# The weights of neighbouring tokens made by VectorE from token rows instead of by TensorE, in a fused RWKV-6 and MLP-mixer kernel

## The chip, the cores and the metric

The kernel runs on one core of a Trainium2 chip. The metric is the device time of one execution in microseconds. Before the change it is 612.65 us, the median of three runs (612.45, 612.65 and 614.34). The profiled execution took 611.08 us and its recorded span is 609.3 us; all times inside the program below are counted from the start of that span.

## What is computed

The reference, cut to what matters. There are 4 batches, 8 heads, 768 tokens and 48 channels for each head; everything is float32.

```python
# attention: state is (B, H, 48, 48)
for t in range(S):
    kt, vt, rt, wt = k[:, :, t], v[:, :, t], r[:, :, t], w[:, :, t]
    cur = einsum('bhd,bhe->bhde', u[None] * kt, vt)      # the own token, weighted by u
    y[:, :, t] = einsum('bhd,bhde->bhe', rt, state + cur)
    state = wt[..., None] * state + einsum('bhd,bhe->bhde', kt, vt)
# then, on x = y laid out as (B, S, 384): the mixer
h  = relu(x^T @ w_tok1) @ w_tok2        # over tokens, 768 -> 256 -> 768
u_ = x + h^T
out = u_ + relu(u_ @ w_ch1) @ w_ch2     # over channels, 384 -> 1536 -> 384
```

The recurrence is computed in chunks of 64 tokens. Within a chunk the output of token t is a weighted sum of the values of the tokens up to t. The weight of an earlier token s is the sum over channels of r at t, k at s and the decays between them; the weight of the token itself is the sum of r, u and k of this token.

## The kernel before

The work is cut into 12 units of 256 tokens, three for each batch. A unit has 2 blocks of 128 tokens (c), each with two chunks of 64 (j), and 4 pairs of heads (a, with q for the two heads of a pair). r, k and w come in turned: the channels of the two heads of a pair lie on partitions 0 to 47 and 64 to 111, and the tokens run along the free dimension.

The weights within a chunk are made in six levels, with block sizes 1, 2, 4, 8, 16 and 32. At each level TensorE multiplies the left half of every pair of blocks (k) with the right half (r), a copy keeps those results that belong to the level, and `join` multiplies the decays into r and k, so that the next level can work with blocks twice as large. The first level is special: it also makes the weight of each token with itself, for which ScalarE first writes copies of r and k, half of whose columns are multiplied by u.

```python
def begin():                                  # ScalarE: rp, kp
    ...
    for t, x, o in both:
        act.copy(t[:, :, o], x[:, :, o])                                    # L226
    for t, x, o in both:
        ...
        for a in range(A):
            act.mul(t[:, :, a, :], x[:, :, a, :], u_col[:ROWS, a:a + 1])    # L230

def gram0(c): ...                             # L242: products of kp and rp in 64 x 64 tiles
def pick0(c):                                 # L248: VectorE keeps the blocks of two
    dve.copy_predicated(out=at_c[:, :, c, :, :], data=g, mask=masks[0]...)

def join(l, w, new):
    ...
    dve.tensor_mul(left, left, wv[:, :, 1]...to_broadcast([ROWS, n, b]))    # L297, k
    dve.tensor_mul(right, right, wv[:, :, 0]...to_broadcast([ROWS, n, b]))  # L298, r
    dve.tensor_mul(new[:ROWS], wv[:, :, 0], wv[:, :, 1])                    # L299

def first_block():
    join(0, products[0], products[1])
    for c in range(UC):
        gram0(c)
        pick0(c)

def block(l):                                 # l = 1 to 5
    gram(l)                                   # L265 (L259 for the last)
    join(l, products[l], products[l + 1])
    pick(l)                                   # L281 on VectorE, L276 and L289 on ScalarE
```

When the weights of a unit are there, `post` finishes it: `tokens` turns k with TensorE (L331), `carry` makes the products of k and v of each chunk (L341), `update` carries the state from chunk to chunk, `before` multiplies r with the states (L378), `within` multiplies the weights with v (L391).

```python
def update():
    ...
    for c in range(UC):
        for j in range(2):
            ...
            if g == 0:
                dve.tensor_copy(new, got)
            else:
                for a in range(A):
                    dve.scalar_tensor_tensor(new[:, a], state[bt, g][:, a], L["w"][:, c, a, j:j + 1],
                                             got[:, a], op0=ALU.mult, op1=ALU.add)      # L358
```

The mixer of one batch runs beside the attention of the next: its full-size products (L429, L436, L456, L490) are woven with the pieces of the attention in the order of TensorE. `beside` says which of the small products of two units go behind each other; the levels run one unit ahead.

```python
return [(1.0, begin[1]), tokens, one(carry, first), update, one(before, rest[0]), one(within, rest[1]),
        *loads, *rest[2:]]
```

Of the kernel before, what the change touches and what calls it, by code (L numbers as in the profile page):

```python
# [10 lines left out]
f32 = mybir.dt.float32  # L11
# [4 lines left out]
ALU = mybir.AluOpType  # L16
AF = mybir.ActivationFunctionType

B, H, S, D = 4, 8, 768, 48
DM = H * D  # L20
T = 64
C = S // 128
UC = 2
UB = C // UC
NU = B * UB
A = H // 2
P = 64
ROWS = P + D
LEVELS = 6
COLS = UC * A * 128  # L30
DTOK, DCH = 256, 1536
NJ = DCH // 128
PIECE = 512
SEG = 256
HJ, HM = NJ // 2, DM // 2
# [19 lines left out]
def rwkv6_then_mixer(  # L55
    ctx: ExitStack,
    tc: tile.TileContext,
    rkw: bass.AP,
    v: bass.AP,
    u: bass.AP,  # L60
    w_tok1: bass.AP,
    w_tok2: bass.AP,
    w_ch1: bass.AP,
# [15 lines left out]
    pe, dve, act, pool, sp = nc.tensor, nc.vector, nc.scalar, nc.gpsimd, nc.sync  # L79

    block = nc.cur_bb.bb
# [17 lines left out]
    ps_m = ctx.enter_context(tc.tile_pool(name="ps_m", bufs=2, space=bass.MemoryType.PSUM))  # L99


    rs = [const.tile([128, COLS], f32, name=f"r{i}") for i in range(3)]
    ks = [const.tile([128, COLS], f32, name=f"k{i}") for i in range(3)]
    ws = [const.tile([128, COLS], f32, name=f"w{i}") for i in range(3)]
    weights_at = [const.tile([128, 2, UC * A, T], f32, name=f"at{i}") for i in range(3)]
    vs = {}
# [1 line left out]
    def load_rkw(i):  # L108
        if i >= NU:
            return  # L110
        for n, t in enumerate((rs[i % 3], ks[i % 3], ws[i % 3])):
            for rows in (slice(0, 128),) if i < 3 else (slice(0, D), slice(P, P + D)):
                sp.dma_start(t[rows], rkw[i, n, rows, :])
# [7 lines left out]

    u_col = const.tile([128, A], f32, name="u_col")
    act.dma_start(u_col, u)
    load_rkw(0)
    load_rkw(1)

# [2 lines left out]
    masks = []  # L129
    for l in range(4):  # L130
        b = 1 << l
        m = const.tile([128, 64 // b, 2 if l == 0 else b], f32, name=f"mask{l}")
        pool.memset(m, 1.0)
        pool.affine_select(out=m, in_=m, compare_op=ALU.is_ge, fill=0.0, base=0,
                           pattern=[[-2 * b, 64 // b], [0, m.shape[2]]], channel_multiplier=1)
        pool.affine_select(out=m, in_=m, compare_op=ALU.is_ge, fill=0.0, base=b - 1,
                           pattern=[[2 * b, 64 // b], [1 if l == 0 else 0, m.shape[2]]], channel_multiplier=-1)
        n, x = (T, 1) if l == 0 else (32, UC * A)
        m8 = const.tile([128, x, n], u8, name=f"mask8_{l}")
        flat = m.rearrange("p n b -> p (n b)")  # L140
        for j in range(2):
            dve.tensor_copy(m8[ts(j, T)], flat[ts(j, T), ts(j, n)].unsqueeze(1).to_broadcast([T, x, n]))
        masks.append(m8)
    for i, t in enumerate(weights_at):
        (dve if i == 0 else pool).memset(t, 0.0)
    ident = const.tile([128, 128], f32, name="ident")
# [56 lines left out]
    state = {}  # L203


    def levels(i):
# [7 lines left out]
        def begin():  # L214
            decay = apool.tile([128, COLS // 2], f32, name="decay")
            L["w"] = apool.tile([128, UC, A, 2], f32, name="w_chunk", bufs=4)
            pool.memset(L["w"], 0.0)
            products.extend([w_, decay, w_[:, :COLS // 4], decay[:, :COLS // 8], w_[:, :COLS // 16],
                             decay[:, :COLS // 32], L["w"].rearrange("p c a j -> p (c a j)")])

            rp = L["rp"] = apool.tile([128, COLS], f32, name="rp")
            kp = L["kp"] = apool.tile([128, COLS], f32, name="kp", bufs=1)
            both = [(t.rearrange("p (n two) -> p n two", two=2)[:ROWS], x.rearrange("p (n two) -> p n two", two=2)[:ROWS], o)
                    for t, x, o in ((rp, r_, 1), (kp, k_, 0))]
# [3 lines that stand above are left out]
                t, x = (e[:, :, 1 - o].rearrange("p (c a n) -> p c a n", c=UC, a=A) for e in (t, x))  # L228
                for a in range(A):
                    act.mul(t[:, :, a, :], x[:, :, a, :], u_col[:ROWS, a:a + 1])  # L230
# [60 lines left out]
        def join(l, w, new):  # L291
            b = 1 << l
            n = COLS // (2 * b)
            right = r_.rearrange("p (n two b) -> p n two b", two=2, b=b)[:ROWS, :, 1, :]
            left = k_.rearrange("p (n two b) -> p n two b", two=2, b=b)[:ROWS, :, 0, :]
            wv = w.rearrange("p (n two) -> p n two", two=2)[:ROWS]
            dve.tensor_mul(left, left, wv[:, :, 1].unsqueeze(2).to_broadcast([ROWS, n, b]))  # L297
            dve.tensor_mul(right, right, wv[:, :, 0].unsqueeze(2).to_broadcast([ROWS, n, b]))  # L298
            dve.tensor_mul(new[:ROWS], wv[:, :, 0], wv[:, :, 1])  # L299

        def first_block():
# [7 lines left out]
            join(l, products[l], products[l + 1])  # L309
            pick(l)  # L310

        pieces = [(0.1, begin), (1.6, first_block)]
        for l in range(1, LEVELS):
            pieces.append((1.2, lambda l=l: block(l)))
        return pieces

    def post(i):
        bt, half = divmod(i, UB)
# [25 lines left out]
        def update():  # L344
            L = live[i]
            kv = L.pop("kv")
            for c in range(UC):
                for j in range(2):
                    g = 2 * (half * UC + c) + j
                    if g == 2 * C - 1:  # L350
                        continue
                    new = apool.tile([128, A, D], f32, name="state", bufs=6)
                    got = kv[:, j, ds(c * A * D, A * D)].rearrange("p (a e) -> p a e", a=A)
                    if g == 0:
                        dve.tensor_copy(new, got)
                    else:
                        for a in range(A):
                            dve.scalar_tensor_tensor(new[:, a], state[bt, g][:, a], L["w"][:, c, a, j:j + 1], got[:, a],  # L358
                                                     op0=ALU.mult, op1=ALU.add)
                    state[bt, g + 1] = new  # L360


# [177 lines left out]
        downs = [first if (bt, s) == (0, 0) else quarters(s) for s in range(S // SEG)]  # L540
        return hiddens, turned, ups, downs

    def beside(after, ahead):

        tokens, carry, update, before, within, *loads = after
        begin, first, *rest = ahead

        def both(f, g):
            behind = products(f)[-1].name
            for ins in products(g):  # L550
                tc.add_manual_dep(ins, behind, no_sync, reason="products in tiles together")

        def one(*pieces):
            return (sum(c for c, _ in pieces), lambda: both(*(f for _, f in pieces)))


        return [(1.0, begin[1]), tokens, one(carry, first), update, one(before, rest[0]), one(within, rest[1]),
                *loads, *rest[2:]]


    hiddens, turned, ups, downs = mixing(0)
# [16 lines left out]
    for bt in range(B):  # L578
# [13 lines left out]
        if n < NU:  # L592
            att = levels(n) if bt == 0 else []
            for i in range(n, n + UB):
                att += beside(post(i), levels(i + 1)) if i + 1 < NU else post(i)
            emit(woven(att, pieces))
        else:
            emit(pieces)
# [29 lines left out]
```

## Time and profile before

| What | Value |
|---|---|
| time, median of three runs | 612.65 us |
| span of the profiled execution | 609.3 us |
| TensorE busy | 578.8 us |
| VectorE busy | 341.1 us |
| ScalarE busy | 201.1 us |
| first level on TensorE (L242) | 18.0 us busy, 768 records |
| copies and u-scalings on ScalarE (L226, L230) | 48.2 us busy |
| state steps on VectorE (L358) | 30.8 us busy, 160 operations |

The page of a profile gives the busy time of each engine, then the same in 40 equal slices, where each digit is the busy share of a slice in tenths. A row of the list of groups names the line, the engine, the operation, what it writes and reads, the shapes and the number of records; behind the bar stand the busy time in us, the mean of one in ns, and the time the engine stood idle before these operations, with what ended it. A float32 product leaves two records on TensorE. The chain that ended last is followed back from the last instruction: its pieces are what set the end. PE is TensorE's products, PEld its weight loads, DVE is VectorE, ACT ScalarE, POOL GpSimd and SP SyncE, which issues the loads. A busy TensorE is not one at its peak, because the ends of products are modelled.

### The profile page before, as it was taken

To read this page: it belongs to the slowest core of one execution; us is meant where nothing else is said; L and a number is where in the kernel's file an instruction comes from. 1 tells how busy PE (TensorE), PEld (TensorE's weight loads), DVE (VectorE), ACT (ScalarE), POOL (GpSimd) and SP (SyncE) were. 2 spreads that over 40 slices of the span, in tenths; PEclk is the share of its full clock that TensorE was granted. 3 is DMA by queue.
4 is the path that set the end of the run, shared out by engine and by line. 5 is a ranking of instruction groups with operands and counts; after the bars stand their busy time and mean duration, and the time that the engine had idled before them with its cause. 6 is when DMAs were issued, how large, how long until landed. Compare 5 with 4: busy or idle time off the path is not lost.

```text
span 609.3 us, 19865 instructions
## 1 busy us (share of the span) xinstructions
PE 578.8 (95%) x8980; PEld 493.9 (81%) x8980; DVE 341.1 (56%) x743; ACT 201.1 (33%) x500; POOL 7.2 (1%) x32
## 2 busy tenths in 40 slices
PE   3888789999999999999999999999999999999997
PEld 2776567877988886789899896789898896898987
DVE  5889989997666873546364362626254431040403
ACT  6153654530354433442333412332212411303020
POOL 4000000000000000000000000000000000000000
PEclk9997869999999999999999999999999999999999
DMA  8336563610322222111121000000000000000000
GB/s 344 117 81 219 176 191 139 210 65 29 79 84 79 55 68 67 30 52 28 54 54 54 29 28 27 2 2 3 27 2 28 2 28 0 1 14 15 26 1 26
DMA packets 19380, 38.63 MB, mean 63 GB/s; under 512 B 2112, under 2 KB 12864, under 8 KB 19296
## 3 DMA queue, kind: packets, MB, share of 16 engines
q1 hardware_dynamic: 19152, 37.36, 19.0%
q8 instruction: 70, 1.15, 0.8%
q14 instruction: 14, 0.11, 0.1%
q10 hardware_dynamic: 144, 0.00, 0.0%
HBM read 32.64 MB, written 4.72 MB: 61 GB/s over the span
## 4 chain that ended last, share of the span: by engine, by line
PE 85%; DVE 8%; ACT 3%; issue 2%; DMA 1%; SPq 0%; DVEq 0%; ACTq 0%
PE z_ps L456 28%; PE q_ps L490 24%; PE gram L265 8%; PE h_ps L429 6%; PE h_ps L436 5%; PE h_ps L466 3%; PE kv_ps L341 2%; PE y_ps L391 2%; PE y_ps L378 2%; PE gram L331 2%; DVE state L358 2%; PE xT_ps L448 1%; PE gram L242 1%; PE gram L259 1%; DMA w<-in_rkw_dram 1%
## 5 line engine op out<-in xcount | busy, mean ns | idle before, releaser
L456 PE MATMUL z_ps<-xT,wch 128*128 128x256 f32 x864 | 196.1, 382 | 0.1
L456 PEld LDWEIGHTS z_ps<-xT,wch 128*128 128x128 f32 x864 | 160.9, 190 | 22.2 <-ACT z L458 1.0
L458 ACT ACTIVATE z<-z_ps 128x256 f32<-128x256 f32 x144 | 54.9, 382 | 149.4 <-PE z_ps L456 140.5
L490 PE MATMUL q_ps<-wch,z 128*128 128x192 f32 x528 | 94.8, 329 | 0.0
L490 PEld LDWEIGHTS q_ps<-wch,z 128*128 128x128 f32 x528 | 86.1, 190 | 1.4
L265 PEld LDWEIGHTS gram<-r,k 48*64 48x64 f32 x3072 | 59.5, 153 | 13.8 <-issue 7.5
L490 PE MATMUL q_ps<-scratch,z 128*128 128x192 f32 x396 | 70.6, 329 | 0.0
L265 PE MATMUL gram<-r,k 48*64 48x32 f32 x3072 | 64.5, 235 | 5.7 <-issue 2.6
L490 PEld LDWEIGHTS q_ps<-scratch,z 128*128 128x128 f32 x396 | 64.4, 190 | 0.5
L297 DVE TENSOR_TENSOR k<-k,decay 112x512 f32<-112x512 f32 x36 | 24.9, 691 | 44.3 <-PE gram L265 34.5
L482 DVE TENSOR_TENSOR z<-z 128x768 f32<-128x768 f32 x11 | 10.5, 958 | 60.6 <-ACT z L458 60.6
L297 DVE TENSOR_TENSOR k<-k,w 112x512 f32<-112x512 f32 x36 | 24.8, 689 | 34.3 <-PE gram L265 28.8
L358 DVE SCALAR_TENSOR_TENSOR state<-state,w_chunk,kv_ps 128x48 f32<-128x48 f32 x160 | 30.8, 256 | 19.9 <-PE kv_ps L341 19.8
L429 PE MATMUL h_ps<-x,wtok 128*128 128x384 f32 x96 | 37.8, 539 | 1.7 <-ACT x L397 1.6
L436 PE MATMUL h_ps<-h,wtok 128*128 128x384 f32 x96 | 35.5, 493 | 0.1
L438 DVE TENSOR_TENSOR x<-x,h_ps 128x384 f32<-128x384 f32 x24 | 13.3, 554 | 38.2 <-PE h_ps L436 37.7
L281 DVE COPY_PREDICATED at<-mask,gram 128x512 f32<-128x512 uint8 x36 | 32.3, 898 | 0.0
L289 ACT COPY at<-gram 16x256 f32<-16x256 f32 x48 | 17.4, 363 | 37.0 <-PE gram L265 35.8
L429 PEld LDWEIGHTS h_ps<-x,wtok 128*128 128x128 f32 x96 | 19.0, 210 | 12.7 <-issue 2.3
L242 PE MATMUL gram<-rp,kp 48*64 48x64 f32 x768 | 18.0, 245 | 10.8 <-ACT kp L230 8.1
L298 DVE TENSOR_TENSOR r<-r,w 112x512 f32<-112x512 f32 x36 | 24.6, 686 | 4.7 <-ACT rp L226 4.7
L242 PEld LDWEIGHTS gram<-rp,kp 48*64 48x64 f32 x768 | 15.9, 154 | 12.6 <-ACT kp L230 10.6
(77 smaller groups left out, 549.4 us busy)
## 6 DMA issues: line engine op xcount, KB each, us to landing
scratch<-in_w_ch_dram SPq DMA_DIRECT2D x10, 512.0 KB, 4.6
vt<-in_v_dram SPq DMA_DIRECT2D x12, 384.0 KB, 4.2
out_dram<-o SPq DMA_DIRECT2D x24, 192.0 KB, 1.9
x<-in_w_ch_dram SPq DMA_DIRECT2D x8, 512.0 KB, 4.4
w<-in_rkw_dram SPq DMA_DIRECT2D x18, 192.0 KB, 3.2
k<-in_rkw_dram SPq DMA_DIRECT2D x18, 192.0 KB, 3.1
r<-in_rkw_dram SPq DMA_DIRECT2D x18, 192.0 KB, 3.5
scratch<-in_w_tok_dram SPq DMA_DIRECT2D x4, 512.0 KB, 9.2
```

Source lines behind the costliest of these rows:

```text
L242: pe.matmul(g[cols, q, ts(a, T)], L["kp"][rows, tokens], L["rp"][rows, tokens], start=True, stop=True)
L265: fours(lambda q, j, rows, cols: pe.matmul(g[cols, q, ts(ca, 32)], k_[rows, ds(ca * 128 + j * T, T)], right[rows, ts(2 * ca + j, 32 // b), ...
L281: dve.copy_predicated(out=dst, data=g.rearrange("p q (m b) -> p q m b", b=b), mask=masks[l].rearrange("p x t -> p (x t)").rearrange("p (m ...
L297: dve.tensor_mul(left, left, wv[:, :, 1].unsqueeze(2).to_broadcast([ROWS, n, b]))
L298: dve.tensor_mul(right, right, wv[:, :, 0].unsqueeze(2).to_broadcast([ROWS, n, b]))
L358: dve.scalar_tensor_tensor(new[:, a], state[bt, g][:, a], L["w"][:, c, a, j:j + 1], got[:, a], op0=ALU.mult, op1=ALU.add)
L429: pe.matmul(sums[i], wtok1[:, c, ts(i, 128)], xs[bt][:, c, :], start=(c == 0), stop=(c == C - 1))
L436: pe.matmul(ps, wtok2[:, i, ts(c, 128)], h1[:, i, :], start=(i == 0), stop=(i == DTOK // 128 - 1))
L456: pe.matmul(ps, wch1[:, m, ts(jt, 128)], xT[:, m, ts(s, SEG)], start=(m == 0), stop=(m == DM // 128 - 1))
L458: act.activation(zs[s][:, jt, :], ps, AF.Relu)
L466: pe.matmul(ps, zs[0][:, jt, ts(n, 128)], wch2[:, jt, :], start=(jt == 0), stop=(jt == NJ - 1))
L490: pe.matmul(ps, a[:, j, :], b[:, j, :], start=(j == 0), stop=(j == HJ - 1))
```

## The change

From the third batch on (units 6 to 11) the weights of the first level are made by VectorE. It reads r, k and "the r of the following token" (zero for odd tokens) as rows of tokens: one token on each partition, 8 x 48 channels along the free dimension. It multiplies r and the following r with k, multiplies the first of them with u, and sums over the 48 channels of each head. `place` writes these sums at the two places in the weights of the chunk that belong to the token: with itself and, for even tokens, with the following one. For these units the copies of r and k on ScalarE, the first products on TensorE and their two masked copies end; `begin` does the first join at once, and the five other levels move one place forward among the pieces of `post`.

Two other things change. From unit 3 on `join` multiplies r and k in one operation, for which the two tiles become halves of one. From the second batch on a state step is one multiplication and one addition over all four pairs of heads, instead of four operations on 48 elements each. The first batch keeps its earlier form in both.

The aim is to take work in small tiles from TensorE, and to make the remaining steps of VectorE fewer and wider.

The diff, cut to its core:

```diff
+NEAR = 2 * UB
-    rs = [const.tile([128, COLS], f32, name=f"r{i}") for i in range(3)]
-    ks = [const.tile([128, COLS], f32, name=f"k{i}") for i in range(3)]
+    rks = [const.tile([128, 2 * COLS], f32, name=f"rk{i}") for i in range(3)]
+    rs, ks = ([t[:, ts(n, COLS)] for t in rks] for n in range(2))
 ...                                                     # in begin()
+            if i >= NEAR:
+                join(0, products[0], products[1])
+                return
 ...                                                     # in join()
-            dve.tensor_mul(left, left, wv[:, :, 1].unsqueeze(2).to_broadcast([ROWS, n, b]))
-            dve.tensor_mul(right, right, wv[:, :, 0].unsqueeze(2).to_broadcast([ROWS, n, b]))
+            rk = rks[i % 3][:ROWS, b:]
+            if i < UB:
+                ...                                      # two multiplications, as before
+            halves = bass.AP(rk.tensor, rk.offset, [list(rk.ap[0]), [COLS - b, 2], [2 * b, n], [1, b]])
+            by = w.rearrange("p (n two) -> p two n", two=2)[:ROWS].unsqueeze(3).to_broadcast([ROWS, 2, n, b])
+            dve.tensor_mul(halves, halves, by)
 ...
-        pieces = [(0.1, begin), (1.6, first_block)]
+        pieces = [(0.1, begin)] + ([(1.6, first_block)] if i < NEAR else [])
 ...
+    def load_near(i):
+        L = near_by[i] = [apool.tile([128, COLS], f32, name="kp", bufs=1)]
+        for c in range(UC):
+            t = apool.tile([128, COLS], f32, name="rp")
+            sp.dma_start(t[:, :2 * DM].rearrange("p (two e) -> p two e", two=2), near[i - NEAR, c, :, :2, :])
+            sp.dma_start(L[0][:, ts(c, DM)], near[i - NEAR, c, :, 2, :])
+    def nearest(i):
+        def row(c):
+            dve.tensor_mul(rr, rr, k.unsqueeze(1).to_broadcast([128, 2, DM]))
+            dve.tensor_mul(rr[:, 0], rr[:, 0], u_rows)
+            dve.tensor_reduce(out=sums[0][:, c], in_=t[:, :2 * DM].rearrange("p (h e) -> p h e", e=D),
+                              axis=mybir.AxisListType.X, op=ALU.add)
+        def place():
+            for q in range(2):
+                dve.tensor_copy(v[:, q, :, :, 0], own[:, q])
+                dve.scalar_tensor_tensor(v[:, q, :, :, 1], own[:, q], odd, later[:, q], op0=ALU.mult, op1=ALU.add)
+            dve.copy_predicated(out=weights_at[i % 3]..., data=two..., mask=masks[0]...)
+        return [(0.3, lambda: row(0)), (0.3, lambda: row(1)), (0.2, lambda: (place(), load_near(i + 1)))]
 ...                                                     # in update()
-                        for a in range(A):
-                            dve.scalar_tensor_tensor(new[:, a], state[bt, g][:, a], ...)
+                        if bt == 0:
+                            ...                          # as before
+                        dve.tensor_mul(new, state[bt, g], L["w"][:, c, :, j].unsqueeze(2).to_broadcast([128, A, D]))
+                        dve.tensor_add(new, new, got)
 ...                                                     # in beside()
+        row0, row1, place = nearest(i + 1)
-        return [(1.0, begin[1]), tokens, one(carry, first), update, one(before, rest[0]), one(within, rest[1]),
-                *loads, *rest[2:]]
+        return [(1.0, begin[1]), tokens, one(carry, rest[0]), update, one(before, rest[1]), row0, one(within, rest[2]),
+                *loads, row1, *rest[3:], place]
```

The pieces of a program are written in this order, and a scheduler then orders the instructions of each engine[...]. The tiles "rp" (two buffers) and "kp" (one) that held ScalarE's copies now also hold the loaded rows.

## Prediction
> **What bounds the kernel now.** I read the page's busy shares and slices first. They name the engine and show whether that holds all the way.
>
> ```profile
> PE 578.8 (95%) x8980; PEld 493.9 (81%) x8980; DVE 341.1 (56%) x743; ACT 201.1 (33%) x500; POOL 7.2 (1%) x32
> PE   3888789999999999999999999999999999999997
> DVE  5889989997666873546364362626254431040403
> ```
>
> A slice is 609.3/40 = 15.2 us. TensorE is full from the seventh slice on. VectorE, at 56% overall, is nearly full in slices 1 to 8 and again at 6 to 8 tenths in slices 10 to 14 (152 to 228 us): an average that hides a crowded part. The table of stretches confirms it, its columns being stretch, length, then busy time of PE, PEld, DVE, ACT and POOL, clock, DMA share and GB/s:
>
> ```profile
> 184.00:205.00 21.00, 20.80 (x572) 17.67 (x564) 16.07 (x39) 10.89 (x30) 0.11 (x1) 1.00 0.23 62
> 205.00:229.00 24.00, 22.79 (x640) 20.92 (x639) 19.45 (x46) 8.14 (x21) 0.11 (x1) 1.00 0.24 65
> 229.00:240.00 11.00, 11.00 (x87) 6.63 (x88) 2.54 (x4) 3.60 (x8) 0.00 (x0) 1.00 0.26 82
> 240.00:263.00 23.00, 22.97 (x452) 17.67 (x446) 12.54 (x31) 10.07 (x26) 0.11 (x1) 1.00 0.13 37
> 263.00:367.00 104.00, 104.00 (x1743) 94.95 (x1737) 55.96 (x122) 33.65 (x89) 0.11 (x1) 1.00 0.14 42
> ```
>
> After 229 us TensorE has no idle time to speak of; VectorE is half free there. Before it, VectorE has 4.6 of 24 us free. Last the chain that ended last (start, us, what), in an undisturbed part:
>
> ```profile
> 284.21 1.08 PE kv_ps L341 x64
> 285.29 0.95 PE gram L242 x64
> 286.24 4.10 PE q_ps L490 x24
> 290.34 3.88 PE z_ps L456 x18
> ...
> 304.92 4.08 PE z_ps L456 x18
> 309.00 1.06 PE gram L265 x64
> 310.06 1.49 PE z_ps L456 x6
> ```
>
> The first block's products (L242) lie on the chain: 0.95 us per unit of 256 tokens, behind another group in small tiles. A group standing alone between full-size products costs 1.06 us, and the full-size products behind it 0.20 us more (4.08 against 3.88 for the same 18). So an entry into small tiles costs (1.06 - 0.95) + 0.20 = 0.31 us beside the work.
>
> [...]690 ns for N = 512, 554 for 384, 958 for 768. No reduction is in this trace, so I take the same form as an estimate: 957 ns for 768. [...]here 192 KB loads land 3.1 to 3.5 us after issue and 384 KB loads 4.2.
>
> **The change part by part.**
>
> *TensorE.* Units 6 to 11 lose their first block: 6 x 0.95 = 5.7 us. Their remaining five blocks move up: block 2 joins the carry, 4 the "before" products, 8 the "within" products, and only 16 and 32 stand alone instead of three. In the instruction order of the built kernels the switches between full and small tiles fall from 127 to 113, 7 entries: 7 x 0.31 = 2.2 us. Together **7.9 us**, all on the chain if nothing else comes to hold it.
>
> *ScalarE.* The copies and u-scalings of r and k end for these units. L226 and L230 take 8.1 + 8.0 + 16.0 + 16.1 = 48.2 us for twelve units, so 24.1 us go: 201 to 177. ScalarE is not the bound; next to nothing of it comes back.
>
> *VectorE, removed.*
>
> ```profile
> L358 DVE SCALAR_TENSOR_TENSOR state<-state,w_chunk,kv_ps 128x48 f32<-128x48 f32 x160 | 30.8, 256 | 19.9 <-PE kv_ps L341 19.8
> L297 DVE TENSOR_TENSOR k<-k,w 112x512 f32<-112x512 f32 x36 | 24.8, 689 | 34.3 <-PE gram L265 28.8
> L298 DVE TENSOR_TENSOR r<-r,w 112x512 f32<-112x512 f32 x36 | 24.6, 686 | 4.7 <-ACT rp L226 4.7
> L248 DVE COPY_PREDICATED at<-mask,gram 128x512 f32<-128x512 uint8 x24 | 17.2, 726 | 1.4 <-PE gram L242 1.4
> ```
>
> In each row "busy, mean ns" is followed by the idle time before it. Per unit the two masked copies of L248 go: 2 x 0.726 = 1.45 us (6 units). A join's two multiplies (0.689 + 0.686 = 1.375) become one of 1024 elements[...]: 0.15 saved, six times a unit, units 3 to 11: 9 x 0.9 = 8 us. A state step of four short operations (4 x 0.256 = 1.02) becomes two of 192 elements, 0.355 each by the 192-element rows of this trace: 0.31 saved, 30 steps: 9.3 us. Removed: 8.7 + 8 + 9.3 = 26 us.
>
> *VectorE, added.* Per row: 0.958 (multiply, 768) + 0.555 (u, 384) + 0.957 (sum, estimate) = 2.47, two rows 4.94. Placing: four operations on 8 elements, 0.17 each by the 16-element row of L299, 0.7; one masked copy of 1024 elements, 1.3 us if it goes like L248, 2.4 if it goes like the worst form of L281 (1.30 us for 512). Sum 6.9 to 8.0, say 7.4 us a unit, 45 us in all. **VectorE ends near 341 - 26 + 45 = 360 us.**
>
> *Beside other work or on the path?* Spread over 184 to 501 us, 45 us would find room: VectorE is idle for about half of that. But the order in the built kernel's VectorE queue isn't spread. The row operations depend on loads only, so they have been put as early as buffers allow: all twelve rows stand between the state updates of unit 4 (about 188 us) and the third block of unit 7 (about 260 us). The worst place is 205 to 229. There the queue gains five first multiplies, four second ones, four sums, eight short operations and the masked copy: 4.8 + 2.2 + 3.8 + 1.4 + 1.8 = 14 us, against 3.2 removed (1.45 + 5 x 0.15 + 3 x 0.31) and 4.6 free. Some 6 us too much. They can slide into the free 8.5 us of 229 to 240, but only behind state steps and joins that TensorE waits for. Walking the queue: behind the carry, y_ps of unit 5 needs three state steps, and among them now stand a sum, a join, a masked copy and a multiply, 7 us where the earlier chain took 3.8 (209.59 to 213.41). Each block up to 32 then waits for a join with 1 to 2 us of row work ahead of it. From 240 to 263, 10.5 us come into 10.5 free ones, with two rows that wait for a load begun only when the row before released its buffer (1 to 2 us each). I put the lost TensorE time at 1 to 8 us, centrally 4. From 265 us on nothing is left of the rows but the placing, and the gain of units 8 to 11 is clean: 4 x 1.26 = 5 us.
>
> *The wide state steps on the chain.* In units 3 to 5 the chain runs through L358; three to four steps at 0.31 in two units with other work beside them give about 0.3 us.
>
> *Transfers.* Each new unit loads 2 x (393 + 197) KB = 1.2 MB, 7 MB in all; the DMA share is 0.13 to 0.26 there. Bandwidth is no limit.
>
> **Sum: 612.65 - 7.9 - 0.3 + 3.6 = 608.0 us** (the 3.6 is my central 4 with a little back from ScalarE).
>
> **The rivals.**
> 1. *TensorE time comes off one for one.* For it: 100% TensorE after 229 us, and half of VectorE free. Against it: the front-loaded queue. It would give 604.5.
> 2. *VectorE becomes the bound from 205 to 263 us and takes nearly all back.* For it: 19.45 of 24 us busy already[...]; the chain there already passes through L358, L248 and L297. Against: most of the excess can slide into 229 to 240, where TensorE's products need nothing from VectorE. It would give 610 to 613.
> 3. *A new wait for loads takes the place of ScalarE's.* Row operations wait for transfers that wait for earlier rows, and the u row is loaded behind other loads in SyncE's queue. For it: 3 to 4 us to landing. Against: two buffers, and other work between most rows. Alone it would cost 1 to 3 us, giving 606 to 608, and it adds to rival 2.
>
> **Range and chances.** 603.5 is the full TensorE gain and some from smoother ScalarE and joins; 612.5 is nearly all taken back. To be faster by over 2% it would have to go under 600.4, more than TensorE loses: 0.03. To be slower by over 2%, above 624.9, the stretch would have to lose 20 us: 0.02. Within 2%: 0.95.
>
> **What would show it.** L242's successor has 384 records instead of 768; TensorE busy falls by about 8 us less what new waits stretch. VectorE busy near 360, ScalarE near 177. The one-operation join takes 1.22 us, the sum 0.96, the masked copy 1.3 to 2.4. On the chain from 263 us to the end no first block, and each of units 8 to 11 shorter by 1.26 us. In 205 to 240 VectorE over 85% busy, and TensorE waiting there for state and join operations, 1 to 8 us more than now. The prediction is wrong if that stretch isn't longer (then 604 to 605),[...] or if waits for VectorE appear after 265 us.

## The result and the profile after

The changed kernel takes **609.26 us**, the median of six runs (608.34 to 610.51), against 612.55 us for the kernel before in the same comparison (six runs, 611.15 to 614.34). The ratio is 0.9946 with a 95% interval of 0.9924 to 0.9969: 0.5% faster, so within 2%, and 1.3 us above the predicted 608.0. The total came out about as predicted; how it is made up did not.

Page of the changed kernel: busy times, then the slices of VectorE and of the granted TensorE clock.

```profile
PE 578.5 (95%) x8596; PEld 493.5 (81%) x8596; DVE 362.6 (60%) x685; ACT 180.1 (30%) x440; POOL 7.2 (1%) x32
...
DVE  5888889998786998876545463526253432040403
...
PEclk9999779999999998999999999999999999999999
```

The clock's row of the kernel before:

```profile
PEclk9997869999999999999999999999999999999999
```

VectorE has 362.6 us, where 360 were expected, and ScalarE 180.1 (177). VectorE's slices 14 to 18, counted from one (198 to 274 us), now stand at 9, 9, 8, 8, 7; before, they were 8, 7, 3, 5, 4. (The prediction counted VectorE's slices from zero.) A new digit is in the clock's row: an 8 in slice 16 (228 to 243 us). The same stretches as before, by the table of stretches (stretch, length, busy PE, PEld, DVE, ACT, POOL, clock, DMA share, GB/s):

```profile
184.00:205.00 21.00, 19.48 (x563) 16.60 (x562) 15.87 (x27) 5.71 (x15) 0.11 (x1) 1.00 0.51 144
205.00:229.00 24.00, 21.56 (x511) 19.85 (x510) 23.90 (x47) 5.42 (x14) 0.11 (x1) 0.93 0.50 134
229.00:240.00 11.00, 11.00 (x160) 8.23 (x159) 8.68 (x14) 3.99 (x10) 0.00 (x0) 0.84 0.46 145
240.00:263.00 23.00, 22.65 (x318) 15.85 (x317) 20.21 (x38) 5.27 (x12) 0.11 (x1) 1.00 0.48 139
263.00:367.00 104.00, 104.00 (x1680) 95.02 (x1683) 57.43 (x103) 27.86 (x71) 0.11 (x1) 1.00 0.17 48
```

VectorE is busy for 23.90 of 24 us in the stretch that was named as the worst place. TensorE's idle time over the first four rows is 1.52 + 2.44 + 0 + 0.35 = 4.3 us against 1.4 us before. The clock, 1.00 in all five rows before, is 0.93 and 0.84 in two of them.

What VectorE's new operations cost, from the groups between 144 and 610 us (behind the bar: busy us, mean ns, idle before):

```profile
L317 DVE TENSOR_TENSOR rk<-rk,decay 112x1024 f32<-112x1024 f32 x26 | 31.8, 1222 | 27.1 <-PE gram L276 16.7 <-PE gram L270 10.2
...
L357 DVE TENSOR_TENSOR rp<-rp,kp 128x768 f32<-128x768 f32 x12 | 11.4, 954 | 3.1 <-DMA rp<-in_near_dram 1.7 <-DMA kp<-in_near_dram 1.4
L359 DVE TENSOR_REDUCE sums<-rp 128x16 f32<-128x768 f32 x12 | 11.3, 949 | 0.1
...
L370 DVE COPY_PREDICATED at<-mask,two 128x1024 f32<-128x1024 uint8 x6 | 7.9, 1311 | 1.6 <-ACT at L287 1.5
```

The join of 1024 elements (L317) takes 1222 ns, the product of a row (L357) 954, its sum (L359) 949, the wide state step (L435 and L436) 2 x 0.36 us, and the masked copy of 1024 elements (L370) 1311 ns, the lower end of its estimate. On TensorE the first level has 384 records instead of 768 (the 32 products of each of 12 units left 768 before, two for each).

Last the chain that ended last (start, us, what), where it is new:

```profile
223.03 0.88 DVE rp L357
223.93 0.56 DVE rp L358
224.49 1.15 DVE rk L317
225.68 1.91 PE gram L276 x64
227.59 4.78 PE q_ps L567 x14
232.37 1.18 PE gram L276 x64
```

From 208 to 226 us all the longer pieces of the chain are VectorE's: a row's product and its u stand ahead of the join that TensorE waits for. Then come 14 records of full-size products in 4.78 us, 0.34 us each; in the kernel before, 12 took 2.15 us at this place, 0.18 each:

```profile
226.19 2.15 PE q_ps L490 x12
```

The records of TensorE itself became slower. Where the first level is gone, the changed kernel's chain is:

```profile
289.14 1.08 PE kv_ps L413 x64
290.22 0.93 PE gram L276 x63
```

Behind the carry of unit 7 stands the block of size 2, in the place where the first level (L242) stood. It joins the carry without an entry of its own, as the prediction had it.

To see where time goes, I read the start of each unit's carry (the kv_ps products) in every trace. From run to run the first 180 us differ by up to 3.9 us (see the runs of unchanged kernels below), so the traces are compared from the carry of unit 4 on. The last three columns are differences of the rounded times:

| Kernel | carry of unit 4 | carry of unit 8 | end | 4 to 8 | 8 to end | 4 to end |
|---|---|---|---|---|---|---|
| before | 182.9 | 330.8 | 609.3 | 147.9 | 278.6 | 426.4 |
| before, again | 182.6 | 330.3 | 608.9 | 147.7 | 278.6 | 426.3 |
| after | 185.1 | 334.4 | 607.9 | 149.3 | 273.5 | 422.9 |
| after, again | 186.5 | 336.0 | 609.6 | 149.5 | 273.6 | 423.1 |
| rows kept in their own unit | 183.7 | 328.3 | 601.9 | 144.6 | 273.6 | 418.2 |
| rows later still | 184.0 | 328.7 | 602.7 | 144.7 | 274.0 | 418.7 |
| wide steps only | 185.2 | 333.6 | 612.1 | 148.4 | 278.5 | 426.9 |
| rows only | 185.8 | 339.9 | 613.2 | 154.0 | 273.4 | 427.4 |
| rows in the last batch only | 184.8 | 334.8 | 606.9 | 150.0 | 272.1 | 422.1 |
| one unit's loads only | 184.6 | 333.8 | 607.2 | 149.2 | 273.4 | 422.6 |

The two repeated kernels agree with their first traces within 0.2 us in these columns. From the carry of unit 8 to the end the change gains 278.6 - 273.5 = 5.1 us. The levels run one unit ahead, so only the first levels of units 9 to 11 lie there: TensorE is busy for 274.0 - 270.2 = 3.8 us less, and 1.2 us of idle time have gone. Between the carries of units 4 and 8 the change loses 1.4 us, although three units (6, 7 and 8) have lost their first level there. So 3.5 us remain, close to the 3.3 us between the medians. Some 0.4 us of them are only moved: two records of z_ps, a product of the mixer (0.2 us each), that the kernel before executes behind the carry of unit 4 stand ahead of it in the changed kernels, except in the one with rows only.

### The profile page after: what moved, and what is told of

Read it like the earlier page. It is cut to its first block, busy times and chain, and to the rows that moved or that the text cites. A ratio compares the mean times of both kernels' runs of the same rounds, so it can differ in the third digit from the quotient of the medians.

```text
span 607.9 us, 18977 instructions
## 1 busy us (share of the span) xinstructions
PE 578.5 (95%) x8596; PEld 493.5 (81%) x8596; DVE 362.6 (60%) x685; ACT 180.1 (30%) x440; POOL 7.2 (1%) x32
## 4 chain that ended last, share of the span: by engine, by line
PE 78%; DVE 15%; issue 2%; ACT 2%; DMA 2%; SPq 0%; DVEq 0%; ACTq 0%
PE z_ps L533 26%; PE q_ps L567 24%; PE gram L276 7%; PE h_ps L506 5%; PE h_ps L513 3%; PE h_ps L543 3%; PE kv_ps L413 2%; PE y_ps L468 2%; PE gram L403 2%; DVE rk L317 2%; PE y_ps L455 2%; DVE wch L192 1%; DVE sums L359 1%; DVE at L292 1%; PE gram L270 1%
## 5 line engine op out<-in xcount | busy, mean ns | idle before, releaser
L567 PE MATMUL q_ps<-wch,z 128*128 128x192 f32 x528 | 97.5, 334 | 0.7 <-DVE o L589 0.7
L567 PEld LDWEIGHTS q_ps<-wch,z 128*128 128x128 f32 x528 | 88.3, 194 | 2.4 <-DVE o L589 1.0
L276 PE MATMUL gram<-rk 48*64 48x32 f32 x3072 | 65.0, 239 | 4.4 <-DVE at L292 1.7
L276 PEld LDWEIGHTS gram<-rk 48*64 48x64 f32 x3072 | 60.6, 158 | 10.5 <-issue 3.8
L317 DVE TENSOR_TENSOR rk<-rk,w 112x1024 f32<-112x1024 f32 x27 | 32.8, 1222 | 30.5 <-PE gram L276 26.8
L317 DVE TENSOR_TENSOR rk<-rk,decay 112x1024 f32<-112x1024 f32 x27 | 33.0, 1222 | 27.1 <-PE gram L276 16.7
L559 DVE TENSOR_TENSOR z<-z 128x768 f32<-128x768 f32 x11 | 10.5, 956 | 61.0 <-ACT z L535 61.0
L513 PEld LDWEIGHTS h_ps<-h,wtok 128*128 128x128 f32 x96 | 16.5, 190 | 9.5 <-ACT h L508 2.6
L287 ACT COPY at<-gram 32x256 f32<-32x256 f32 x48 | 17.4, 363 | 15.1 <-PE gram L270 14.6
L404 ACT COPY kT<-gram 128x512 f32<-128x512 f32 x24 | 14.1, 586 | 26.4 <-PE gram L403 26.2
L436 DVE TENSOR_TENSOR state<-state,kv_ps 128x192 f32<-128x192 f32 x30 | 10.7, 357 | 18.5 <-PE kv_ps L413 18.1
```

What stands on the lines that cost most here:

```text
L276: fours(lambda q, j, rows, cols: pe.matmul(g[cols, q, ts(ca, 32)], k_[rows, ds(ca * 128 + j * T, T)], right[rows, ts(2 * ca + j, 32 // b), ...
L287: act.copy(at[p:p + b, :, ts(c, A), b:], g[ds(p + c * b, b)])
L317: dve.tensor_mul(halves, halves, by)
L404: act.copy(L["kT"][:, c], ps)
L513: pe.matmul(ps, wtok2[:, i, ts(c, 128)], h1[:, i, :], start=(i == 0), stop=(i == DTOK // 128 - 1))
L567: pe.matmul(ps, a[:, j, :], b[:, j, :], start=(j == 0), stop=(j == HJ - 1))
```

## Experiments

My theory was that the order causes the loss: the row operations stand too early in VectorE's queue, and TensorE waits behind them. Rivals were that the row work itself is too much wherever it stands, that the loads hold it up, or that the wide steps change what TensorE waits for.

### Rows kept in their own unit

A dependency without a wait ties the first operation of a row to the last VectorE instruction written ahead of it. The scheduler can then no longer put the rows in front of earlier units' work. Nothing else changes.

```diff
+            mark = next(ins.name for ins in reversed(block.instructions) if ins.engine == dve.engine)
-            dve.tensor_mul(rr, rr, k.unsqueeze(1).to_broadcast([128, 2, DM]))
+            first = dve.tensor_mul(rr, rr, k.unsqueeze(1).to_broadcast([128, 2, DM]))
+            tc.add_manual_dep(first.ins, mark, no_sync, reason="rows in their own unit")
```

> The changed kernel, but each row's first multiplication is held behind the VectorE operation written before it, so that a row runs in its own unit and not as early as buffers allow. Theory (rows crowd VectorE from 205 to 263 us, TensorE waits for joins there and its clock then halves): VectorE busy in 205 to 229 us falls from 23.9 of 24 to about 21, no clock under 0.95 there, and the time is 604.5 to 606.5 us, ratio to before 0.987 to 0.990. Rival (the rows cost TensorE time wherever they stand, or their loads do): 608 to 610 us as in the changed kernel, ratio 0.993 to 0.996.

Measured: **604.66 us** (603.6 to 605.52), ratio to before 0.9851, 95% interval 0.9821 to 0.9882. (Each ratio is taken to runs of the kernel before in the same set. Their median was 613.1 us in this set and 612.9 and 614.7 us in the two later ones, so ratios and not times are to be compared; the quotient of two medians can differ from the ratio by about 0.001.) That is faster than both kernels; the interval doesn't touch that of the change as it was (0.9924 to 0.9969). First a row's sum in the list of one tile's instructions (min/median/max ns, first and last start), in the changed kernel and then with the rows kept in place, where the same operation stands two lines further down:

```profile
L359 DVE TENSOR_REDUCE sums<-rp x12: 944/949/955, 201.1 to 286.4; 128x16 f32<-128x768 f32 x12
```

```profile
L361 DVE TENSOR_REDUCE sums<-rp x12: 946/953/953, 218.9 to 459.5; 128x16 f32<-128x768 f32 x12
```

The same twelve sums are spread over 241 us instead of 85. The stretches with the rows kept in place:

```profile
205.00:229.00 24.00, 22.00 (x578) 20.04 (x576) 20.95 (x37) 4.93 (x13) 0.11 (x1) 1.00 0.27 78
229.00:240.00 11.00, 11.00 (x89) 6.64 (x92) 5.59 (x11) 3.60 (x8) 0.00 (x0) 1.00 0.57 170
```

VectorE's total hardly differs (363.4 us against 362.6), so the amount of work isn't what costs: its place is. TensorE is idle for 2.9 us from 184 to 263 us against 4.3, and the clock stays at 1.00. From the carry of unit 4 the two differ by 422.9 - 418.2 = 4.7 us: 1.4 us less idle time, and the rest where the clock falls.

### Where the clock falls

The same stretch in steps of 3 us, the changed kernel:

```profile
223.00:226.00 3.00, 1.35 (x70) 1.10 (x63) 2.97 (x5) 0.48 (x1) 0.00 (x0) 0.96 0.71 187
226.00:229.00 3.00, 3.00 (x65) 2.94 (x62) 3.00 (x5) 0.95 (x3) 0.00 (x0) 0.50 0.84 212
229.00:232.00 3.00, 3.00 (x11) 2.86 (x9) 2.79 (x6) 0.00 (x0) 0.00 (x0) 0.50 0.77 264
232.00:235.00 3.00, 3.00 (x72) 2.27 (x71) 1.38 (x2) 1.35 (x4) 0.00 (x0) 0.90 0.20 71
```

TensorE is idle for 1.65 us in the first row; in the next two the clock is at half. TensorE's list around this wait (start, us, what, and in brackets the idle time before it and its releaser):

```profile
225.14 0.33 PE L468 MATMUL y_ps<-vt,at 64*64 64x48 f32 x7 [1.43 <-issue]
225.68 1.91 PE L276 MATMUL gram<-rk 48*64 48x32 f32 x64 [0.21 <-DVE rk L317]
```

For the longer gap the profile names no releaser ("issue"). What set the time is read from the chain: the block's products (L276) start at 225.68 us, when the join (L317) ends, whatever the seven records before them do. A stretch of 3 us at 0.96 has been at half for 0.24 us, one at 0.90 for 0.6 us: together 0.24 + 3 + 3 + 0.6 = 6.8 us at half, nearly all of it busy, which costs 3.4 us. With the 1.4 us of added idle time that makes 4.8 us, and 4.7 were to be explained.

That the clock falls because of the wait was so far an inference. I tried to make such a wait in the kernel before, which has no gap of more than 0.8 us from 187 us to its last product: first with needless multiplications ahead of a join of unit 8.

```diff
+            if i == 8 and l == 2:
+                for _ in range(6):                       # 10 in the second run
+                    dve.tensor_scalar(k_[:ROWS], k_[:ROWS], 1.0, None, op0=ALU.mult)
```

> The kernel before, with six multiplications of k by 1.0 on VectorE ahead of the third join of unit 8, near 305 us, where TensorE has no idle time. Each should take 0.69 us, together about 3.7 us; the join has some 2.7 us to spare. Theory: a wait of about 1 us is lost once and the clock stays at 1.0, so the end moves by about 1 us. Rival (any wait halves the clock): a stretch at 0.5 follows and costs some 3 us more.

> The same with ten multiplications, 6.4 us and a wait of about 3.5 us on TensorE. Theory (a wait of some microseconds makes the clock fall to half for some 6 us, as in the changed kernel after 226 us): the clock in 3 us stretches shows 0.5 behind the wait, and the interval from the carry of unit 8 to that of unit 9 grows from 49.7 us by 3.5 + 3 = 6.5. Rival (the low clock in the changed kernel had another cause): no clock under 0.95, and the interval grows by 3.5 us.

Measured: spans of 613.5 and 613.6 us. Both runs start late (carry of unit 4 at 186.5 and 186.3 us). The interval that I had named, from the carry of unit 8 to that of unit 9, is 49.64 and 49.65 us against 49.71 in the kernel before, but it can't show the wait: the joins of unit 8 run one unit ahead, and the extra operations (from 309 us on) lie ahead of the carry of unit 8 at 335 us. From the carry of unit 7 to that of unit 8 it is 46.72 and 47.53 us against 46.61. With six operations TensorE didn't wait at all, as other products had been put in between. With ten, the waits of TensorE from 310 to 330 us were:

```profile
PE gram L265 <- DVE k L297: 0.9, 1, 0.9
```

The clock stayed at 1.00, and the interval grew by 0.9 us, the wait alone. That is a miss for the purpose: the disturbance was too small. It does show that this wait of 0.9 us wasn't enough. So the next pair put the operations where TensorE has nothing else left, ahead of the last state of the mixer's channel part in the last batch, near 563 us:

```diff
+                if (bt, s) == (B - 1, 1):
+                    for _ in range(12):                  # 16 in the second run
+                        dve.tensor_scalar(s1, s1, 1.0, None, op0=ALU.mult)
```

> The kernel before with twelve extra VectorE multiplications by 1.0 ahead of the last state of the last batch (near 563 us, where TensorE has no other product left to do). Theory that the granted clock falls behind a wait of TensorE: TensorE waits some 3 us at that state, the granted clock reads about 0.5 in a 3 us window just behind it (it read 1.00 there before), the products of that window take about twice their time, and the end is later by the wait and by some 1 to 3 us more: span about 613 to 615 us against 609. Rival, that the clock fell for another reason: the clock stays at 1.00 behind the wait and the end is later by the wait alone, span about 612 us.

> As with twelve multiplications, but sixteen: a wait of some 5 us. Theory: the clock falls to 0.5 behind it, for as long as or longer than with twelve, and the end is later by the wait and 2 to 4 us more: span about 616 to 618 us. Rival: the clock stays at 1.00 and the span is about 614 us.

Measured: spans of 617.0 and 620.9 us. TensorE waits once, for 4.0 and 6.4 us. With twelve operations:

```profile
570.00:573.00 3.00, 0.00 (x0) 0.00 (x0) 2.88 (x6) 0.00 (x0) 0.00 (x0) 0.88 0.00 0
573.00:576.00 3.00, 2.37 (x7) 2.37 (x8) 2.47 (x3) 0.00 (x0) 0.00 (x0) 0.50 0.00 0
576.00:579.00 3.00, 3.00 (x11) 3.00 (x11) 0.55 (x1) 0.00 (x0) 0.00 (x0) 0.50 0.00 0
579.00:582.00 3.00, 3.00 (x20) 3.00 (x19) 0.71 (x2) 0.00 (x0) 0.00 (x0) 0.98 0.00 0
```

The products behind the wait come 11 to a row instead of 20. The fall begins within the wait and again lasts 0.7 + 3 + 3 + 0.1 = 6.8 us. From the last carry product to the end it is 617.0 - 488.7 = 128.3 us against 608.9 - 487.6 = 121.3 in the kernel before (repeated run): 7.0 us, of which 4.0 are the wait; of the other 3.0 the clock explains 2.8, since TensorE was busy for 5.5 us at half speed. With sixteen operations, 620.9 - 491.3 = 129.6 us: 8.3 us more, 6.4 of them the wait. Of the other 1.9 the clock explains 1.7: half of its 6.8 us at half speed passed while TensorE still waited. So in these two runs a wait of 4.0 and one of 6.4 us did bring the clock from 1.00 to 0.50, and the rival (the wait alone) is out. Both waits made here are longer than the 1.65 us in question, though. For waits as short as that there is no wait made for the purpose, only the falls that followed them, counted next, and the absence of a fall where the rows are spread. The sizes were missed upward: the waits were 4.0 and 6.4 us, not 3 and 5, and these two spans also contain what their starts differ by.

How much waiting is enough? In each trace I summed TensorE's idle time over the 3.4 us (the length of the shortest of these falls) ahead of every point from 187 to 265 us. Where the clock fell, it was 1.65 us in the changed kernel, 1.65 in its repetition, 1.2 with one unit's loads, and 1.3 and 2.6 in the two falls with rows only. Where the sum never exceeded 1.0 us (before 0.7, rows in place 0.6, rows later 1.0), there was no fall. Three spots with 1.1 to 1.3 us had none either (near 203 and 249 us with one unit's loads, near 205 us in the repetition), so this isn't an exact threshold. Nor does it take one long gap: in the changed kernel two gaps of 1.43 and 0.21 us were followed by a fall.

### One unit's loads only

Are the loads what crowds VectorE? The rows of unit 6 are used for units 7 to 11 too and those units' loads are left out, so their first-level weights are not those of the reference; the work of VectorE stays.

```diff
+        if i > NEAR:
+            near_by[i] = near_by[NEAR]
+            return
```

> The changed kernel with the rows of unit 6 used again for units 7 to 11: the loads of those five units are left out (their outputs use unit 6's rows), so that no row waits for a load that waits for an earlier row; their VectorE work and its early place remain. Theory (the work itself crowds VectorE): 608 to 610 us, ratio 0.993 to 0.997. Rival (waits for the loads, 4.4 us on VectorE in the changed kernel, are the cause): 604 to 606 us, ratio 0.986 to 0.989.

Measured: 609.19 us, ratio 0.995 (0.9927 to 0.9974), the same as the change with its loads.

```profile
223.00:226.00 3.00, 2.10 (x68) 1.94 (x69) 3.00 (x9) 1.43 (x3) 0.00 (x0) 0.89 0.51 145
226.00:229.00 3.00, 3.00 (x11) 2.81 (x9) 2.62 (x5) 0.00 (x0) 0.00 (x0) 0.54 0.17 59
```

VectorE is still full, and the clock still falls, here for 3.4 us, which costs 1.7. TensorE's idle time from 184 to 263 us is 5.8 us where it was 4.3, so the two together come to 7.5 us against 7.7. The test is not a full one: the loads of unit 6 and of the row of u remain, and VectorE still waits 2.8 us for them, where it waited 4.1 us for rows and u in the changed kernel. With the rows kept in their own unit it waits for none, so that run alone doesn't tell loads and work apart. But the waits of the changed kernel lie at 190 to 200 us and at 266 us. From 205 to 229 us, ahead of the fall and into it, VectorE was busy for 23.90 of 24 us and waited for no load. There the loads aren't the cause; the rows' own time is.

### Wide steps only, and rows only

Two kernels take the change apart. In the first no unit uses rows (the first level stays on TensorE); in the second the rows stay, but joins and state steps keep their old form everywhere.

```diff
-NEAR = 2 * UB
+NEAR = NU                # wide steps only
 ...                      # u's row isn't loaded; the input arrays stay as they were
```

```diff
-            if i < UB:
+            if True:         # rows only: the old join
-                        if bt == 0:
+                        if True:     # and the old state step
```

> Only the other two parts: joins in one operation from unit 3 on and wide state steps from the second batch on, no rows; every first block stays on TensorE. Theory: VectorE falls by about 17 us (8 joins, 9.3 states), next to nothing of it on the path: 612.0 to 612.5 us, ratio 0.998 to 1.0. Rival (these parts gave the 3 us, rows gave nothing): 609 to 610 us, ratio 0.995.

> Only the rows: two multiplications for each join and four operations for each state step, as before. Theory (crowding): VectorE has about 2 us more to do in 205 to 229 us, so TensorE waits 1 to 3 us longer than in the changed kernel: 610 to 612 us, ratio 0.996 to 1.0. Rival (joins and states don't matter): 609 to 609.5 us, ratio 0.995.

Measured: wide steps only 612.86 us, ratio 0.9981 (0.9964 to 0.9998); rows only 612.3 us, ratio 0.9976 (0.9957 to 0.9996). Each alone is worth next to nothing. Both times lie 0.3 to 0.4 us above what was expected, both ratios within it. The first lines of the pages, wide steps first:

```profile
PE 582.9 (95%) x8980; PEld 496.8 (81%) x8980; DVE 336.0 (55%) x629; ACT 201.4 (33%) x500; POOL 7.2 (1%) x32
```

```profile
PE 579.8 (95%) x8596; PEld 493.7 (81%) x8596; DVE 368.9 (60%) x799; ACT 179.9 (29%) x440; POOL 7.2 (1%) x32
```

The wide steps save VectorE 341.1 - 336.0 = 5.1 us, and 368.9 - 362.6 = 6.3 when the rows are there; the prediction had 17. The state steps alone took 30.8 us before and take at most 28.4 with wide steps only (10.6 + 10.5 + 7.3, by their lines): 2.4 us less, where 9.3 were expected. On TensorE's path they bring nothing of their own (426.9 us from unit 4 to the end against 426.4). With rows only, the gain from unit 8 to the end is the same 5 us, but units 4 to 8 take 154.0 us. TensorE waits there more than with the whole change; its longest waits from 187 to 350 us:

```profile
PE xT_ps L525 <- DVE x L515: 3.9, 2, 2.6
PE gram L276 <- DVE rk L312: 2.4, 3, 1.3
```

The clock falls twice, near 206 and 254 us, for 3.4 us each time. Against the rows kept in place, the idle time from 187 to 350 us is 7.7 us instead of 2.9, and 3.4 us go to the clock: 8.2 of the 9.2 us between the two; 0.4 more are the two records of z_ps. So in this trace the wide steps do matter, by the room they leave in the crowd, not by their own time on the path. The times show it less clearly: the 22 runs with rows only spread from 606.96 to 618.42 us, the one traced (614.89) is above their median, and the interval of the ratio overlaps that of the whole change (0.9924 to 0.9969). Whether both falls come in every run isn't shown.

### Rows in the last batch only

```diff
-NEAR = 2 * UB
+NEAR = 3 * UB
```

> Rows for units 9 to 11 alone, so that they fall into 280 to 370 us where VectorE is half free. Theory: each unit gives its 1.26 us and nothing is lost: 612.55 - 3.8 - 0.3 = 608.4 us, ratio 0.993, no clock drop after 144 us. It would equal or beat the changed kernel with half of its units. Rival (a unit gives about half a microsecond net wherever it is, as 3.3/6 us suggests): 610.5 to 611 us, ratio 0.997.

Measured: 608.76 us, ratio 0.9916 (0.9883 to 0.9948). Units 6 to 8 keep their first level; the rows now run from 292 to 337 us, still packed together. The clock stays at 1.00 behind 144 us, and TensorE's idle time from 187 to 350 us is 2.6 us. From unit 4 to the end 422.1 us: 3.9 us more than with all rows kept in place, which is three units at 1.3 us. Half of the gain without the fall is worth as much as all of it with the fall.

### Unchanged kernels again

> The kernel before once more, for a second profile of its first 185 us. In the profile shown, the carry of unit 2 starts at 74.1 us and that of unit 4 at 182.9; in the changed kernel and the first four experiments at 76.5 to 78.2 and 183.7 to 185.8. Theory (the start varies from run to run with the granted clock, and the change has no part in it): unit 2 at 76 to 78, unit 4 at 184 to 186. Rival (the change costs 2 us in the start): 74.1 and 182.9 again, within half a microsecond.

> The changed kernel once more, unchanged. If the later start belongs to the kernel as built, the carry of unit 2 begins again within 0.5 us of 77.6 us and that of unit 4 within 0.5 us of 185.1 us. If it differs from run to run, they begin elsewhere, by more than 1 us. Theory of the waits in 205 to 235 us: the clock of about 0.5 near 226 to 232 us comes again, since the crowding of VectorE that leads to it is in the order of the instructions. Rival: the clock is 1.00 there in this run.

The kernel before gave 610.67 us (span 608.9) and began unit 4's carry at 182.6 us, as in its first profile (182.9): that run alone didn't show the start to vary. The changed kernel gave 611.27 us (span 609.6), and its carries of units 2 and 4 began at 79.2 and 186.5 us, against 77.6 and 185.1. So the later start isn't a fixed property of the build. The two kernels with twelve and sixteen operations near 563 us show it most clearly: up to that point their instructions are the same on every engine, and their carries of unit 4 began at 183.1 and 186.3 us. With six and ten operations, which come only at 309 us, they began at 186.5 and 186.3 us. In the first 100 us the clock is at half in stretches of 3.4 to 10.2 us whose places and lengths differ from run to run. Ahead of these stretches it was low as well, though the clock's row shows 9s there: the first change of the clock in the trace is a rise, at 43.3 us in the kernel before and at 61.9 us in the changed one, and the kernel before's products of L265 take 292 ns from 20 to 40 us, against 220 from 100 to 180 us. In the changed kernel the same products (L276) take 291 ns where the row shows 0.50 (226 to 232 us) and 219 where it shows 1.00 (265 to 350 us). If that time is counted as half clock (an estimate), the three runs with 63 to 64 us of it begin unit 4 at 182.6 to 183.7 us, two with 70 us at 183.1 and 186.5, and the nine with 75 to 80 us at 184.0 to 186.5. So the start varies with the clock; what sets it in a given run I can't tell.

The fall behind the waits came again in the repetition: at half from 227.2 to 234.0 us, 6.8 us, behind 1.65 us of idle time. In both traces it comes with this order of the instructions.

### Rows later still

With the rows kept in place, each row may still stand better behind one more block.

```diff
-        return [(1.0, begin[1]), tokens, one(carry, rest[0]), update, one(before, rest[1]), row0, one(within, rest[2]),
-                *loads, row1, *rest[3:], place]
+        if i + 1 < NEAR:
+            return ...                               # units without rows: the order as it was
+        return [(1.0, begin[1]), tokens, one(carry, rest[0]), update, one(before, rest[1]), one(within, rest[2]),
+                *loads, rest[3], row0, rest[4], row1, place]
```

> The rows kept in place as in the version that beat both kernels, but each row multiplication one piece of the unit later, after the third and fourth block pieces. Theory that only their spread counts: the same within its uncertainty or a little faster, 603.5 to 605 us, ratio 0.983 to 0.987 to the kernel before. Rival, that the placement copy then comes too close to the reduction that reads it: TensorE waits on the gram's inputs again in 205 to 235 us, and the time is 606 to 609 us.

Measured: 605.51 us (604.4 to 606.59), ratio 0.9863 (0.9841 to 0.9885), clock 1.00. The time is half a microsecond above what was expected, the ratio within it. It can't be told from the rows kept in place (0.9821 to 0.9882). Once the rows are spread, one block more or less is of no account; the rival's waits didn't come.

## Why the prediction held, and which steps did not

- **TensorE's saving of 7.9 us, and 0.3 for wide state steps: their sum held.** With the rows in place TensorE is busy for 411.9 us from the carry of unit 4 to the end instead of 420.4: 8.5 us less, of which 0.4 are the two records of z_ps that only moved. So 8.1 us were saved. The path is 426.4 - 418.2 = 8.2 us shorter, because two smaller things nearly cancel: 1.5 us more idle time up to 263 us, and 1.2 us of idle time between 350 and 560 us (0.8 behind L248) that went with the first level. This idle time the prediction had overlooked. The 0.3 alone isn't seen: with wide steps only nothing is gained.
- **The clean gain of units 8 to 11 held.** Their first levels lie between the carry of unit 7 and the end. The stretch before and after:

```profile
284.14:609.33 325.19, 320.61 (x3885) 282.94 (x3884) 125.05 (x276) 79.92 (x205) 0.11 (x1) 1.00 0.06 20
```

```profile
289.07:607.91 318.84, 315.49 (x3629) 278.78 (x3628) 121.41 (x221) 71.21 (x180) 0.11 (x1) 1.00 0.06 20
```

TensorE is busy for 320.61 - 315.49 = 5.1 us less, 1.28 for each unit; the prediction had 5.0 and 1.26. The stretch is shorter by 6.4 us, as the 1.2 us of idle time are in it. Row work went on longer than the prediction said, with the last sum at 286 us instead of 265, and cost nothing there: TensorE has no idle time from 265 to 350 us.
- **The place of the loss held:** 205 to 263 us, VectorE in front of TensorE, busy for 32.6 of the 35 us from 205 to 240 (93%).
- **The lost time, "1 to 8 us, centrally 4", lacked a part.** Against the kernel before, TensorE's idle time up to 263 us grew by 2.9 us (4.3 for 1.4), which is within the range. The halved clock behind the wait cost 3.4 us more: 6.3 us in all. Against the spread rows the loss is 4.7 us, 1.4 by waiting and 3.4 by the clock. The step that failed is the walk through the queue, which counted waits at full clock. It also took for granted that in VectorE's queue nothing passes an operation that waits; no run here shows that by itself.
- **That the total came within 1.3 us of 608.0 is in part luck.** From the carry of unit 4 to the end the changed kernel's sum is -8.2 (TensorE's time at full clock) - 0.4 (moved) + 2.9 (waits) + 3.4 (clock) - 1.2 (idle time gone) = -3.5 us. The clock and the idle time that went were both unforeseen and have opposite signs.
- **VectorE's removed 26 us is the mis-sized term.** Joins and state steps save 5.1 us, not 17. I had multiplied means by counts. The row of L358 already spoke against it: 160 x 0.256 is 41 us, its busy time 30.8, since operations behind each other overlap. The chain shows the same: L357 advances it by 0.88 us, though one takes 0.954. The rows came out too dear in the same way: with rows only VectorE grows by 27.8 us, where 45 - 8.7 = 36 were expected. Some 3 us of this are the masked copy, 1.31 us where 1.3 to 2.4 had been allowed; the rest is overlap. The two errors nearly cancelled: +21.5 for +19 us. The lengths of single operations held. The products of before with N = 384, 512 and 768 elements (L438 554 ns, L297 690, L482 958) rise by some 1.05 ns for each further element. For the join of 1024 that gives 1.23 us, an estimate; 1.22 was predicted and 1222 ns were measured, against 1375 for the two operations. The sum was put at 957 ns, about the 958 of a product of its length, and takes 949.
- **Rival 1 (TensorE's time one for one, 8.2 us) is what the change gives when the rows are spread:** 604.66 us against 613.1 in the same set, 8.4 us. **Rival 3 (loads)** has its waits in the trace (1.7 and 1.4 us before L357, 1.0 before L358), but none from 205 to 229 us, and leaving out the loads of five units changed nothing. **Rival 2** was right about the stretch and went too far in the sum.

## What to carry to other kernels

Work moved to an engine with free time on average must also be spread where the scheduler would bunch it: one ordering dependency without a wait brought 4.7 us, more than the change by itself (3.5). In these traces TensorE waited for 1.1 to 2.6 us within 3.4 us in eight places, and in five of them the clock then fell, which cost 1.7 or 3.4 us more; so look at the granted clock in steps of 3 us wherever TensorE idles. For short operations behind each other, take the busy time of the row divided by the count (30.8/160 = 0.19 us for L358), not the mean of one (0.256).

## What the runs showed of the hardware beyond what I expected

- In five places, behind 1.2 to 2.6 us of TensorE idle time within 3.4 us, the granted clock fell from 1.00 to 0.50 for 3.4 or 6.8 us; with up to 1.0 us it didn't, and in three spots with 1.1 to 1.3 us it didn't either. A wait of 4.0 us made on purpose cost 7.0 us, one of 0.9 us only itself.
- Multiplication and sum over 48 channels of 768 elements take the same time (954 and 949 ns).
- Until its first recorded change, at 43 to 63 us here, the clock's row shows full clock although the products of L265 are slow (292 ns in the kernel before, where they later take 220).
- Kernels with the same instructions up to 563 us differed by 3.2 us at 183 us into the run; a single span can't settle a difference of that size here.
